# The end of the attention passes as one explicit list of single steps, with expert 0's early products between them

## The chip, the cores and the metric

The kernel runs on one core of one Trainium2 chip. The metric is the device time of one execution in microseconds (us). The core has five engines that run beside each other, each strictly in the order of its own program: PE (TensorE, matrix products), DVE (VectorE), ACT (ScalarE), POOL (GpSimd, which also issues the indirect DMAs) and SP (SyncE, which issues the other DMAs).

## The reference

```python
def _attn_ref(q, k, v):                       # 8 batches, 8 heads, 576 tokens, 64 features
    ...
    q_d = q.reshape(B, H, Sd, factor, D).mean(axis=3)     # factor 4; k_d and v_d likewise
    out_d = sm_attn(q_d, k_d, v_d)
    out_up = np.repeat(out_d, factor, axis=2)
    mask = np.abs(pos[:, None] - pos[None, :]) < factor
    scores = np.where(mask, scale * np.matmul(q, k.transpose(0, 1, 3, 2)), -1000000000.0)
    ...
    return (out_up + np.matmul(attn, v)).astype(np.float32)

def _moe_ref(x, w_gate, w1, w2):              # x: 4608 tokens of 512 features
    logits = x @ w_gate
    expert_idx = np.argmax(logits, axis=1)    # one of 8 experts
    ...
    for e in range(E):
        h = np.maximum(x_sorted[lo:hi] @ w1[e], 0.0)      # 512 -> 1024
        y_sorted[lo:hi] = h @ w2[e]                       # 1024 -> 512
    return (gate_w[:, None] * y).astype(np.float32)
```

A token attends to its neighbours at a distance below 4 and, on a coarse grid of means over 4 tokens, to all tokens of its batch. The sum of both is the input of a mixture of 8 experts, of which each token takes the one with the highest logit.

## The kernel before

**Attention** takes 32 passes; pass i handles two heads of one batch, four passes make a batch. A pass is cut into steps (local scores `s_loc`, their row maximum `max_loc`, the exponent `exp_loc`, row sums `sums`, `norm`, transposes `t_loc` and `t_d`, their copies out of PSUM `e_loc` and `e_d`, the products with the values `pv_loc` and `pv_d`, `out_d`, and `add_up`, which writes the pass's output into `XT`). The steps of neighbouring passes are interleaved: the table `PASS` holds (step, lag) pairs, and `steps(i)` emits every step for pass i minus its lag. So attention needs three more calls, `steps(32)` to `steps(34)`, to drain, and `steps(35)` for what follows them.

**Routing** works on groups of tiles of 128 tokens; a pair of batches m has nine tiles, taken as the first four (FIRST4) and the last five (LAST5). It runs in three parts: `route_a` (gate logits on PE, `r_mm`, and their copy `r_lg`), `route_b` (turn, maximum, one-hot of the winner) and `route_c` (`r_place` ranks the tokens within their expert on PE, `r_rk`, `r_pos`, then `r_ix` on POOL makes row numbers). `x_rows` transposes a tile of `XT` into token rows and `scatter` sends these with an indirect DMA to the expert's place in `xs` in DRAM.

**Expert 0 starts early.** Its first 256 rows (`EARLY`) are there before the last tokens are routed. They are loaded (`x_load(0, 0)`, four DMAs, L586), transposed on DVE (L617), split into a high part on ACT (L621) and a low part on DVE (L622), and go through the first layer as eight products `s1(0, f, EARLY)`: each has 12 PE instructions (L674 to L676), a copy on ACT (L678) and one on DVE (L679). The second layer needs both halves of w2 (`split_w2`: ACT L663, DVE L664). `s2(0, 0)` and `s2(0, 1)` (L688 to L690) finish the early tokens. The other 256 columns of expert 0, and all that follows, need `x_load(0, 1)`, which reads `xs` after every scatter has landed. While rows are being read from `xs`, no scatter may write it: the scatter behind `x_load(0, 0)` waits for that load.

What sets the order is the order in which the code emits the steps: each engine runs its share of them in that order, and a step that waits holds back all that stands behind it on its engine. PSUM banks set waits too: `bank()` has three, and transposes, logits and ranks share them.

Before the change, `x_load(0, 0)` stands at the end of pass 31; then come `steps(32)`, half of a routing group, two `x_rows`, the split of the early rows, `steps(33)`, the first product, the remaining passes, and then routing, scatters, products and w2 splits in whole functions (the block at the end of the main loop).

Of the kernel before, what the change touches and what calls it, by code (L numbers as in the profile page):

```python
# [90 lines left out]
def attention_moe_kernel(ctx: ExitStack, tc: tile.TileContext, qk, vw, vd, wg, w1, w2, cst, csb, out):  # L91
# [316 lines left out]

    def r_lg(m, tiles):
        lg = RS[m, "lg"] = rp.tile([128, 384], F32, name="over", bufs=1)  # L410
        w = 256 if len(tiles) == 4 else 384
        nc.scalar.activation(lg[:, :w], RS[m, "p"][:, :w], AF.Copy)

    def r_turn(m, tiles):
        lg = RS[m, "lg"]
        p = RS[m, "p"] = bank()
        for u in range(2):
# [5 lines left out]
    def r_max(m, tiles):  # L423
        T = len(tiles)
        RS[m, "pl"] = RS[m, "p"][:, :T * 32].rearrange("p (t e) -> p t e", e=32)[:, :, :E]
        RS[m, "m"] = rp.tile([128, 5], F32, name="rm")
        nc.vector.tensor_reduce(RS[m, "m"][:, :T], RS[m, "pl"], axis=AX.X, op=OP.max)

    def r_sub(m, tiles):
        T = len(tiles)  # L430
        d = RS[m, "d"] = RS[m, "p"][:, 256:296].rearrange("p (t e) -> p t e", e=E)
        nc.vector.tensor_sub(d[:, :T], RS[m, "pl"], RS[m, "m"][:, :T, None].to_broadcast([128, T, E]))

    def r_exp(m, tiles):
        T = len(tiles)
        ex = RS[m, "ex"] = rp.tile([128, 5, E], F32, name="re")
        nc.scalar.activation(ex[:, :T], RS[m, "d"][:, :T], AF.Exp)

    def r_top(m, tiles):
        T = len(tiles)  # L440
        sc = RS[m, "sc"] = RS[m, "p"][:, 320:360].rearrange("p (t e) -> p t e", e=E)
        nc.vector.scalar_tensor_tensor(sc[:, :T], RS[m, "d"][:, :T], 0.0,
                                       cf[:, None, C_DESC:C_DESC + E].to_broadcast([128, T, E]),
                                       op0=OP.is_ge, op1=OP.mult)

    def r_first(m, tiles):
        T = len(tiles)
        nc.vector.tensor_reduce(RS[m, "m"][:, :T], RS[m, "sc"][:, :T], axis=AX.X, op=OP.max)

    def r_hot(m, tiles):  # L450
        T = len(tiles)
        oh = RS[m, "oh"] = rp.tile([128, 5, E], BF, name="oh")
        nc.vector.tensor_tensor(oh[:, :T], RS[m, "sc"][:, :T], RS[m, "m"][:, :T, None].to_broadcast([128, T, E]),
                                op=OP.is_equal)

    def r_gate(m, tiles):
        T = len(tiles)
        gt = RS[m, "gt"] = rp.tile([128, 5], F32, name="gt")
        nc.vector.tensor_reduce(gt[:, :T], RS[m, "ex"][:, :T], axis=AX.X, op=OP.add)

    def r_eps(m, tiles):
        T = len(tiles)
        gt = RS[m, "gt"]
        nc.scalar.activation(gt[:, :T], gt[:, :T], AF.Copy, bias=1e-9)

    def r_place(m, tiles):
        T = len(tiles)
        oh = RS[m, "oh"]
        p = RS[m, "p"] = bank()
        nc.tensor.matmul(p[:, :T * E], trib, oh[:, :T], start=True, stop=False, skip_group_check=True)  # L470
# [6 lines left out]
    def r_cs(m, tiles):  # L477
        cs = RS[m, "cs"] = rp.tile([128, E], F32, name="cs")
        nc.vector.tensor_reduce(cs, RS[m, "oh"][:, :len(tiles)].rearrange("p t e -> p e t"), axis=AX.X, op=OP.add)

    def r_run(m, tiles):
        nc.gpsimd.tensor_add(crun, crun, RS[m, "cs"])

    def r_rk(m, tiles):
        T = len(tiles)
        rk = RS[m, "rk"] = rp.tile([128, 5, E], F32, name="rk", bufs=1)
        nc.vector.tensor_mul(rk[:, :T], RS[m, "p"][:, :T * E].rearrange("p (t e) -> p t e", e=E), RS[m, "oh"][:, :T])

    def r_pos(m, tiles):
        T = len(tiles)  # L490
        pos = RS[m, "pos"] = rp.tile([128, 5], F32, name="pos")
        nc.vector.tensor_reduce(pos[:, :T], RS[m, "rk"][:, :T], axis=AX.X, op=OP.add)

    def r_ix(m, tiles):
        T = len(tiles)
        ix = rp.tile([128, 5], I32, name="ix")
        nc.gpsimd.tensor_copy(ix[:, :T], RS[m, "pos"][:, :T])
        for j, t in enumerate(tiles):
            IDX[m, t] = ix[:, j:j + 1]

    def r_last(m, tiles):
# [3 lines left out]
        nc.scalar.copy(xrs[:, sl, DM + 1], cf[:, C_TOK + t0:C_TOK + t0 + T])  # L505
        nc.vector.reciprocal(xrs[:, sl, DM], RS[m, "gt"][:, :T])

# [11 lines left out]

    def x_rows(m, t):  # L520
        p = bank()
        for k in range(4):
            nc.tensor.transpose(p[:, k * 128:(k + 1) * 128], XT[m][:, k, t * 128:(t + 1) * 128], ident)
        xr = xrs[:, x_slot(m, t)]
        nc.scalar.activation(xr[:, :DM].rearrange("p (b k d) -> p k b d", k=4, d=32),  # L525
                             p.rearrange("p (k b d) -> p k b d", k=4, d=32), AF.Copy)

    prev_sc = []
# [151 lines left out]

# [232 lines left out]
    def steps(i):  # L913
        for f, lag in PASS:
            if 0 <= i - lag < NP:
                f(i - lag)

    load_vd(0)
    steps(-1)
    for i in range(NP):  # L920
        steps(i)
# [40 lines left out]
    x_rows(m, 4)  # L962
    split_w2(0, 0)
    s1(0, 3, EARLY)
    x_rows(m, 5)
    for f in (4, 5, 6, 7):
        s1(0, f, EARLY)
        if f == 4:
            for t in rest:
                scatter(m, t)  # L970
        for j in (2 * f - 7, 2 * f - 6):
            if j < 6:
                split_w2(0, j)
    totals()
    close_pv.close()
# [98 lines left out]
```

## Time and profile before

| | us |
|---|---|
| median of 3 runs | 649.36 |
| lowest and highest | 646.58, 651.08 |
| the profiled execution | 644.67 |
| its span, first to last instruction | 642.9 |
| PE busy, share of the span | 617.6, 96% |

The profile is one execution. Engine rows give start, duration, engine, line and operation. "x8" says that eight instructions in a row are merged. A row of the chain of waits is a piece of the work that ended last, each released by the one above it.

### The profile page before, as it was taken

The page shows a single profiled execution, that of the slowest core. Times are in us where ns is not written, and L with a number is a line of the kernel's source. Part 1 is how long each engine was busy: PE and PEld are TensorE (multiplying, and loading weights), DVE is VectorE, ACT ScalarE, POOL GpSimd, SP SyncE. Part 2 cuts the span into 40 slices and gives each one's busy share as a digit, 9 for nine tenths or more (in the row PEclk, how much of TensorE's full clock was granted, in tenths as well). Part 3 has the DMA queues.
Part 4 walks back from the last instruction along what each step waited for, and adds up shares of the span by engine and source line. Part 5 has one row for each costly group of instructions (what it writes and reads, how often), then busy time and mean ns, then how long its engine had stood idle before and what let it go on. Part 6 is the DMA issues. An engine that isn't in the chain of part 4 may idle for free.

```text
span 642.9 us, 15721 instructions
## 1 busy us (share of the span) xinstructions
PE 617.6 (96%) x6123; PEld 507.9 (79%) x6123; DVE 352.3 (55%) x691; ACT 343.3 (53%) x941; POOL 226.6 (35%) x348
## 2 busy tenths in 40 slices
PE   7899999999979899999999999999999999999994
PEld 4678887787768798888888888888888888888873
DVE  5999988888854573751571174175038166115020
ACT  4899999999964353543452263264235154223120
POOL 7877899999924311111111101101011111110111
PEclk9999999999989999999999999999999999999997
DMA  8998999999862794383274276258137537010001
GB/s 286 286 269 285 292 302 286 292 280 290 239 195 84 187 304 136 122 224 90 84 191 138 66 187 192 68 155 213 56 109 183 181 112 197 35 47 1 34 18 43
DMA packets 68612, 108.65 MB, mean 169 GB/s; under 512 B 15724, under 2 KB 39804, under 8 KB 68496
## 3 DMA queue, kind: packets, MB, share of 16 engines
q1 hardware_dynamic: 62080, 87.78, 49.0%
q0 software_dynamic: 5984, 19.01, 7.9%
q8 instruction: 66, 1.08, 0.8%
q14 instruction: 50, 0.41, 0.2%
q10 hardware_dynamic: 432, 0.37, 0.2%
HBM read 87.09 MB, written 23.67 MB: 172 GB/s over the span
## 4 chain that ended last, share of the span: by engine, by line
PE 68%; issue 10%; POOL 7%; DMA 5%; DVE 5%; ACT 2%; SPq 1%; POOLq 0%; another core or an unknown queue 0%; DVEq 0%; ACTq 0%
PE p L675 8%; PE p L674 8%; PE p L676 8%; PE p L690 7%; PE p L688 7%; PE p L689 7%; POOL xs L550 2%; DMA vd<-in_vd_dram 2%; PE pD L305 2%; POOL vdt L230 2%; PE pX L770 2%; PE pX L789 2%; PE pX L342 1%; PE pS L251 1%; PE pX L329 1%
## 5 line engine op out<-in xcount | busy, mean ns | idle before, releaser
L695 POOL DMA_INDIRECT out_dram<-y,tix x39 | 37.9, 971 | 213.3 <-ACT y L707 201.9
L674 PE MATMUL p<-xh,w1h 128*128 128x512 f32 (+1 forms) x288 | 106.4, 370 | 0.8 <-ACT xh L621 0.7
L675 PE MATMUL p<-xl,w1h 128*128 128x512 f32 (+1 forms) x288 | 105.7, 367 | 0.8 <-DVE xl L622 0.8
L676 PE MATMUL p<-xh,w1l 128*128 128x512 f32 (+1 forms) x288 | 105.5, 366 | 0.0
L688 PE MATMUL p<-w2h,hh 128*128 128x512 f32 x256 | 101.1, 395 | 0.0
L689 PE MATMUL p<-w2l,hh 128*128 128x512 f32 x256 | 99.8, 390 | 0.5 <-DVE w2l L664 0.5
L690 PE MATMUL p<-w2h,hl 128*128 128x512 f32 x256 | 99.9, 390 | 0.0
L679 DVE SCALAR_TENSOR_TENSOR hl<-p,hh 128x512 fp32r<-128x512 f32 (+1 forms) x72 | 45.5, 632 | 94.3 <-ACT hh L678 93.6
L678 ACT ACTIVATE hh<-p 128x512 fp32r<-128x512 f32 (+1 forms) x72 | 39.6, 551 | 78.1 <-PE p L676 75.6
L707 ACT ACTIVATE y<-p,gi 128x512 f32<-128x512 f32 x32 | 22.0, 689 | 91.2 <-PE p L690 86.8
L674 PEld LDWEIGHTS p<-xh,w1h 128*128 128x128 f32 x288 | 54.7, 190 | 10.7 <-ACT xh L621 1.1
L675 PEld LDWEIGHTS p<-xl,w1h 128*128 128x128 f32 x288 | 54.7, 190 | 9.6 <-DVE xl L622 0.9
L676 PEld LDWEIGHTS p<-xh,w1l 128*128 128x128 f32 x288 | 54.6, 190 | 8.7
L689 PEld LDWEIGHTS p<-w2l,hh 128*128 128x128 f32 x256 | 48.1, 188 | 10.6 <-DVE w2l L664 0.9
L690 PEld LDWEIGHTS p<-w2h,hl 128*128 128x128 f32 x256 | 48.1, 188 | 10.2
L688 PEld LDWEIGHTS p<-w2h,hh 128*128 128x128 f32 x256 | 48.1, 188 | 9.5
L664 DVE TENSOR_TENSOR w2l<-raw,w2h 128x512 fp32r<-128x512 f32 x64 | 43.3, 681 | 2.1 <-DMA xs<-xr,ix 1.5
L622 DVE TENSOR_TENSOR xl<-pX,xh 128x512 fp32r<-128x512 f32 x38 | 24.7, 684 | 35.2 <-ACT xh L621 34.2
L194 ACT ACTIVATE w1h<-raw 128x512 fp32r<-128x512 f32 (+1 forms) x72 | 42.1, 584 | 0.0
L550 POOL DMA_INDIRECT xs<-xr,ix x36 | 36.4, 1012 | 15.6 <-ACT xr L525 6.9
L663 ACT ACTIVATE w2h<-raw 128x512 fp32r<-128x512 f32 x64 | 39.8, 626 | 2.8 <-DMA xs<-xr,ix 2.8
L230 POOL TENSOR_TENSOR vdt<-vd 72x512 f32<-72x512 f32 x32 | 40.9, 1279 | 0.3
(152 smaller groups left out, 1240.1 us busy)
## 6 DMA issues: line engine op xcount, KB each, us to landing
raw<-in_w_dram SPq DMA_DIRECT2D x59, 512.0 KB
qk<-in_qk_dram SPq DMA_DIRECT2D x32, 583.0 KB
vw<-in_vw_dram SPq DMA_DIRECT2D x32, 320.0 KB
vd<-in_vd_dram SPq DMA_DIRECT2D x32, 288.0 KB
xrow<-xs SPq DMA_DIRECT2D x32, 192.0 KB
xrow<-xs SPq DMA_DIRECT2D x32, 128.0 KB
xs<-zs SPq DMA_DIRECT2D x6, 512.0 KB
raw<-in_w_dram SPq DMA_DIRECT2D x20, 128.0 KB
```

Source lines behind the costliest of these rows:

```text
L194: nc.scalar.activation(hi[:, s], src[:, s], AF.Copy)
L230: nc.gpsimd.tensor_add(t2, v[:, 0:2], v[:, 2:4])
L550: ins = nc.gpsimd.indirect_dma_start(out=xs, out_offset=bass.IndirectOffsetOnAxis(ap=IDX[m, t], axis=0), in_=xr, in_offset=None)
L663: nc.scalar.activation(hi, src, AF.Copy)
L664: nc.vector.tensor_sub(lo, src, hi)
L674: nc.tensor.matmul(p, wh[:, fs], xh[:, k, r], start=(k == 0), stop=False)
L675: nc.tensor.matmul(p, wh[:, fs], xl[:, k, r], start=False, stop=False)
L676: nc.tensor.matmul(p, wl[:, fs], xh[:, k, r], start=False, stop=(k == 3))
L679: nc.vector.scalar_tensor_tensor(hl[:, f, r], p, 0.0, hh[:, f, r], op0=OP.max, op1=OP.subtract)
L688: nc.tensor.matmul(p, hh, wh, start=(f == 0), stop=False)
L689: nc.tensor.matmul(p, hh, wl, start=False, stop=False)
L690: nc.tensor.matmul(p, hl, wh, start=False, stop=(f == 7))
```

## The change

1. `vw`, the values of a pass, gets three buffers instead of two.
2. `early_count`, which checks that expert 0 already has its 256 early rows, stands behind pass 28 instead of pass 29.
3. The main loop ends after pass 30. All that followed, from pass 31 to `totals`, becomes the table `TAIL` of 195 single steps in one written order. For that, functions that did several engines' work are cut into one step per engine: `x_rows` into `x_tr` (PE) and `x_ev` (ACT), `s1` into `s1_mm` (PE), `s1_hi` (ACT) and `s1_lo` (DVE), `split_w2` into `w2_hi` (ACT) and `w2_lo` (DVE), the split of the early rows into `x_up` (DVE), `x_hi` (ACT) and `x_lo` (DVE). The operations and their sizes stay.
4. The routing's scratch table is keyed by group as well, so that two groups can be under way.

```diff
-        VW[i] = p2.tile([128, NC, 2, D], F32, name="vw", bufs=2)
+        VW[i] = p2.tile([128, NC, 2, D], F32, name="vw", bufs=3)
...
-        p = RS[m, "p"] = bank()
+        p = RS[m, tiles[0], "p"] = bank()
...
-    def x_rows(m, t):
-        p = bank()
+    def x_tr(m, t):
+        p = BX["x", m, t] = bank()
...
+    def s1_mm(f):
+        s1_part(0, f, EARLY, 0)
+
+    def s1_hi(f):
+        s1_part(0, f, EARLY, 1)
+
+    def s1_lo(f):
+        s1_part(0, f, EARLY, 2)
...
+    TAIL = (
+        (max_d, 30), (x_tr, 2, 8), (exp_loc, 30), (eps, 29), (e_d1, 28), (x_tr, 3, 2), (s_loc, 31), (inv, 29),
...
-    for i in range(NP):
+    for i in range(NP - 1):
         steps(i)
...
         if i == 28:
             nc.sync.dma_start(cf[:, C_LIM:], cst[:, C_LIM:])
-        if i == 29:
             early_count()
-        if i == NP - 1:
-            close_p1.close()
-            close_s.close()
-            _, mp[0] = pool(name="m1", bufs=1)
-            _, mp["p1"] = pool(name="psM1", bufs=2, space=PSUM)
-            x_load(0, 0)
-            gi_load(0, 0, 2)
-            raw_ahead(8)
-    m = B // 2 - 1
-    first, rest = list(range(4)), list(range(4, 9))
-
-    steps(NP)
-    route_b(m, first)
-    x_rows(m, 2)
-    x_rows(m, 3)
-    prep(0, 0, 1, get=h_bank)
-    steps(NP + 1)
-    s1(0, 0, EARLY)
-    gi_make(0, 0, 2)
-    steps(NP + 2)
-    steps(NP + 3)
-    route_a(m, rest)
-    route_c(m, first)
-    for t in (2, 3, 0, 1):
-        scatter(m, t)
-    route_b(m, rest)
-    x_rows(m, 6)
-    x_rows(m, 7)
-    s1(0, 1, EARLY)
-    route_c(m, rest)
-    x_rows(m, 8)
-    s1(0, 2, EARLY)
-    x_rows(m, 4)
-    split_w2(0, 0)
-    s1(0, 3, EARLY)
-    x_rows(m, 5)
-    for f in (4, 5, 6, 7):
-        s1(0, f, EARLY)
-        if f == 4:
-            for t in rest:
-                scatter(m, t)
...
-    totals()
+    for f, *a in TAIL:
+        f(*a)
```

Three places show how instructions move. The first is PE, from the values' products of the last pass (L357 and L370) to the logits of LAST5 (L401 and L406) and what stands ahead of its ranks (L470). Before:

```order
L357 MATMUL pPV<-AT,vw 64x58 x20
L370 MATMUL pPV<-ADT,vds 64x144 x4
L401 MATMUL pX<-XT,wgt 32x256 x8
L406 MATMUL pX<-XT,wgt 32x128 x4
L470 LDWEIGHTS cb
L470 MATMUL pX<-oh,cb 128x32
```

Of the change (L697 is the last line of an early product, L676 before):

```order
L697 MATMUL p_4612<-xh_4316,w1l_3643 128x256
L401 MATMUL pX<-XT,wgt 32x256 x8
L406 MATMUL pX<-XT,wgt 32x128 x4
L523 MATMUL pX<-cf,XT 128x128 x4
L418 MATMUL pX<-cf,over 128x64 x2
L421 MATMUL pX<-cf,over 128x32
L523 MATMUL pX<-cf,XT 128x128 x4
```

A whole product stands ahead of the logits now, the ranks of FIRST4 (L470, 128x32) are gone from behind them, and the rows' transposes (L523) stand around the turn (L418).

The second is DVE around the row numbers of LAST5 (L492 before `r_ix`). Before:

```order
L459 TENSOR_REDUCE gt<-re 128x5
L679 SCALAR_TENSOR_TENSOR hl<-p_4629,hh 128x256
L479 TENSOR_REDUCE cs<-oh 128x8
L487 TENSOR_TENSOR rk<-pX,oh 128x40
L492 TENSOR_REDUCE pos<-rk 128x5
L506 RECIPROCAL xr<-gt 128x5
L679 SCALAR_TENSOR_TENSOR hl<-p_4668,hh 128x256
L664 TENSOR_TENSOR w2l_4696<-raw,w2h_4695 128x512
```

Of the change (L701 is L679 before, L677 is L664):

```order
L459 TENSOR_REDUCE gt<-re 128x5
L701 SCALAR_TENSOR_TENSOR hl<-p_4612,hh 128x256
L479 TENSOR_REDUCE cs<-oh 128x8
L487 TENSOR_TENSOR rk<-pX,oh 128x40
L492 TENSOR_REDUCE pos<-rk 128x5
L506 RECIPROCAL xr<-gt 128x5
L701 SCALAR_TENSOR_TENSOR hl<-p_4675,hh 128x256
L677 TENSOR_TENSOR w2l_4699<-raw,w2h_4698 128x512
```

The low part ahead of the ranks belongs to an earlier product now (p_4612 is the product ahead of the logits above), and two low halves of w2 follow instead of six.

The third is POOL between the two groups' row numbers (L497). Before:

```order
L605 CAST tix<-gi 128x2
L497 CAST ix<-pos 128x4
L482 TENSOR_TENSOR crun<-crun,cs 128x8
L549 MEMSET spacer 1x1
L550 DMA xs<-xr,ix 42112x514
```

Of the change (L556 and L557 are the same spacer and scatter):

```order
L612 CAST tix<-gi 128x2
L661 MEMSET tgi 128x2
L661 MEMSET ttix 128x1
L661 MEMSET gap 128x16
L497 CAST ix<-pos 128x4
L482 TENSOR_TENSOR crun<-crun,cs 128x8
L556 MEMSET spacer 1x1
L557 DMA xs<-xr,ix 42112x514
```

Before, two scatters of batch pair 2 stand ahead of L605 and four scatters follow L482; of the change, one stands ahead of L612 and five follow.

## Rows read from the trace of the kernel before

**Rows 1.** The chain of waits in 16 to 50 us: start, duration, what.
```profile
25.37 0.74 DVE mx L264
...
30.11 0.75 DVE mx L264
...
35.03 1.18 ACT AD L319 x6
```

**Rows 2.** Waits in 16 to 50 us: total, times, longest.
```profile
POOL qkt L219 <- DMA qk<-in_qk_dram: 6.5, 5, 1.8
```

**Rows 3.** SP's waits in 16 to 50 us.
```profile
SPq L211 <- PE pPV L357: 13.1, 5, 3.0
```

**Rows 4.** Busy time by stretch: PE, PEld, DVE, ACT, POOL, granted clock, DMA share, GB/s.
```profile
182.00:184.00 2.00, 0.82 (x8) 0.62 (x8) 1.09 (x7) 0.38 (x3) 0.00 (x0) 1.00 1.07 138
...
188.00:190.00 2.00, 1.90 (x11) 1.90 (x12) 0.83 (x2) 1.40 (x5) 0.00 (x0) 0.62 1.04 399
190.00:192.00 2.00, 2.00 (x12) 2.00 (x11) 0.00 (x0) 0.53 (x1) 0.00 (x0) 0.53 0.30 116
...
200.40:223.50 23.10, 22.41 (x143) 19.37 (x141) 11.40 (x30) 10.40 (x24) 10.27 (x22) 1.00 0.61 160
```

**Rows 5.** The chain of waits in 165 to 226 us.
```profile
167.52 0.60 PE pPV L357 x39
168.12 0.65 PE pPV L370 x8
168.77 0.69 PE pX L329 x5
169.47 0.44 PE pX L523 x4
...
195.05 0.84 DVE XT L385 x2
...
206.02 1.36 POOL xs L550
...
212.00 3.29 DMA xs<-xr,ix
...
217.03 4.92 DMA xrow<-xs
```

**Rows 6.** PE in order of time, pieces of 189 to 226 us.
```profile
190.13 0.56 PE L674 MATMUL p<-xh,w1h 128*128 128x256 f32 x1
...
192.43 0.45 PE L342 MATMUL pX<-cf,AD 112*72 112x112 f32 x3
...
196.39 0.39 PE L406 MATMUL pX<-XT,wgt 128*32 128x128 f32 x4
...
198.91 0.36 PE L674 MATMUL p<-xh,w1h 128*128 128x256 f32 x1
...
200.42 0.19 PE L470 MATMUL pX<-oh,cb 128*128 128x40 bf16 x1
...
223.04 0.39 PE L690 MATMUL p<-w2h,hl 128*128 128x512 f32 x1
...
225.22 0.38 PE L675 MATMUL p<-xl,w1h 128*128 128x256 f32 x1 [0.75 <-DVE xl L622]
```

**Rows 7.** DVE in order of time: the early rows' transposes.
```profile
183.97 1.32 DVE L617 STREAM_TRANSPOSE p<-xrow 128x512 f32<-128x512 f32 x2 [0.19 <-DMA xrow<-xs]
```

**Rows 8.** ACT in order of time, pieces of 179 to 197 us.
```profile
185.00 1.08 ACT L621 ACTIVATE xh<-p 128x512 fp32r<-128x512 f32 x2
...
194.61 0.41 ACT L374 ACTIVATE outd<-pPV 128x288 f32<-128x288 f32 x1 [0.96 <-PE pPV L370]
```

**Rows 9.** POOL in order of time, pieces of 201 to 204 us.
```profile
201.20 0.97 POOL L550 DMA_INDIRECT xs<-xr,ix  x1 [0.22 <-issue]
202.48 0.97 POOL L550 DMA_INDIRECT xs<-xr,ix  x1 [0.22 <-DVE xr L506]
203.46 0.20 POOL L497 CAST ix<-pos 128x5 int32<-128x5 f32 x1
```

More of the change, by code (lines that the diff above doesn't have):

```diff
@@ L467, in r_place @@
         T = len(tiles)
-        oh = RS[m, "oh"]
-        p = RS[m, "p"] = bank()
+        oh = RS[m, tiles[0], "oh"]
+        p = RS[m, tiles[0], "p"] = bank()
         nc.tensor.matmul(p[:, :T * E], trib, oh[:, :T], start=True, stop=False, skip_group_check=True)
@@ L526, in x_rows @@
                              p.rearrange("p (k b d) -> p k b d", k=4, d=32), AF.Copy)
+    def x_rows(m, t):
+        x_tr(m, t)
+        x_ev(m, t)
     prev_sc = []
@@ L916, in steps, with shut, x_in, gi_in @@
                 f(i - lag)
+    XP = {}
+    def shut():
+        close_p1.close()
+        close_s.close()
+        _, mp[0] = pool(name="m1", bufs=1)
+        _, mp["p1"] = pool(name="psM1", bufs=2, space=PSUM)
+    def x_in():
+        x_load(0, 0)
+        XH[0, 0] = tuple(mp[0].tile([128, 4, FIRST], F32R, name=f"x{w}0") for w in "hl")
+        HT[0] = tuple(mp[0].tile([128, 8, FIRST], F32R, name=f"h{w}") for w in "hl")
+    def gi_in():
+        gi_load(0, 0, 2)
+    def w2_in():
+        raw_ahead(8)
@@ new lines, in s1_lo, with w2_hi, w2_lo @@
+    def s1_lo(f):
+        s1_part(0, f, EARLY, 2)
+    def w2_hi(f):
+        w2_open(0, f)
+        w2_part(0, f, 0)
+    def w2_lo(f):
+        w2_part(0, f, 1)
+    TAIL = (
+        (max_d, 30), (x_tr, 2, 8), (exp_loc, 30), (eps, 29), (e_d1, 28), (x_tr, 3, 2), (s_loc, 31), (inv, 29),
+        (r_mm, 3, FIRST4), (x_ev, 2, 8), (t_d0, 28), (max_scale, 30), (x_ev, 3, 2), (norm, 29), (inv_d, 29),
+        (x_tr, 2, 7), (exp_d, 30), (max_loc, 31), (s_d, 31), (sub_loc, 31), (norm_d, 29), (r_lg, 3, FIRST4),
+        (r_turn, 3, FIRST4), (x_ev, 2, 7), (sums, 30), (exp_loc, 31), (x_tr, 3, 3), (pv_loc, 28), (r_max, 3, FIRST4),
+        (pool_v2, 30), (scatter, 2, 6), (e_d0, 28), (max_d, 31), (pool_v, 31), (pool_v2, 31), (shut,), (x_in,),
+        (r_sub, 3, FIRST4), (pv_d, 28), (r_top, 3, FIRST4), (eps, 30), (inv_d, 30), (x_ev, 3, 3), (inv, 30),
+        (norm_d, 30), (r_first, 3, FIRST4), (r_hot, 3, FIRST4), (t_loc1, 29), (e_loc1, 29), (norm, 30), (gi_in,),
+        (r_place, 3, FIRST4), (r_rk, 3, FIRST4), (t_d1, 29), (out_d, 28), (t_d0, 29), (x_up, 1), (add_up, 28),
+        (e_d1, 29), (e_d0, 29), (t_d1, 30), (e_d1, 30), (x_up, 0), (x_hi, 1), (x_lo, 1), (scatter, 2, 8), (ld_vw, 30),
+        (t_loc0, 29), (t_d0, 30), (r_pos, 3, FIRST4), (max_scale, 31), (e_loc0, 29), (e_d0, 30), (x_hi, 0), (x_lo, 0),
+        (t_loc1, 30), (exp_d, 31), (pv_d, 29), (pv_loc, 29), (t_loc0, 30), (out_d, 29), (w2_in,), (r_exp, 3, FIRST4),
+        (sums, 31), (gi_out,), (e_loc0, 30), (x_tr, 3, 1), (eps, 31), (e_loc1, 30), (inv, 31), (inv_d, 31),
+        (x_ev, 3, 1), (r_ix, 3, FIRST4), (norm_d, 31), (s1_mm, 2), (w2_hi, 0), (norm, 31), (s1_hi, 2), (s1_mm, 3),
+        (add_up, 29), (t_loc1, 31), (e_loc1, 31), (t_loc0, 31), (r_cs, 3, FIRST4), (r_gate, 3, FIRST4), (pv_d, 30),
+        (r_eps, 3, FIRST4), (out_d, 30), (s1_lo, 2), (e_loc0, 31), (s1_hi, 3), (pv_loc, 30), (x_tr, 3, 0), (t_d0, 31),
+        (r_run, 3, FIRST4), (t_d1, 31), (e_d0, 31), (scatter, 2, 7), (r_last, 3, FIRST4), (e_d1, 31), (ld_vw, 31),
+        (add_up, 30), (pv_loc, 31), (x_ev, 3, 0), (w2_lo, 0), (pv_d, 31), (out_d, 31), (scatter, 3, 0), (add_up, 31),
+        (w2_hi, 2), (w2_lo, 2), (w2_hi, 5), (s1_lo, 3), (s1_mm, 6), (w2_hi, 1), (scatter, 3, 3), (r_mm, 3, LAST5),
+        (w2_lo, 1), (w2_hi, 4), (r_lg, 3, LAST5), (x_tr, 3, 5), (x_ev, 3, 5), (w2_lo, 5), (r_turn, 3, LAST5),
+        (r_max, 3, LAST5), (r_sub, 3, LAST5), (scatter, 3, 2), (s1_hi, 6), (r_top, 3, LAST5), (r_first, 3, LAST5),
+        (r_hot, 3, LAST5), (x_tr, 3, 8), (s1_mm, 0), (r_exp, 3, LAST5), (r_gate, 3, LAST5), (x_ev, 3, 8), (s1_lo, 6),
+        (scatter, 3, 1), (r_cs, 3, LAST5), (w2_hi, 3), (r_place, 3, LAST5), (r_eps, 3, LAST5), (r_rk, 3, LAST5),
+        (r_run, 3, LAST5), (r_pos, 3, LAST5), (r_ix, 3, LAST5), (s1_hi, 0), (r_last, 3, LAST5), (s1_lo, 0),
+        (w2_lo, 3), (w2_lo, 4), (x_tr, 3, 4), (x_ev, 3, 4), (s1_mm, 5), (s1_hi, 5), (s1_mm, 1), (s1_lo, 5),
+        (scatter, 3, 5), (x_tr, 3, 7), (s1_hi, 1), (x_ev, 3, 7), (s1_lo, 1), (x_tr, 3, 6), (s1_mm, 4),
+        (scatter, 3, 4), (x_ev, 3, 6), (s1_mm, 7), (scatter, 3, 8), (scatter, 3, 7), (s1_hi, 4), (totals,),
+        (s1_lo, 4), (s1_hi, 7), (s1_lo, 7), (scatter, 3, 6),
+    )
```

118 lines of the change are left out of this document (70 added, 48 removed).

## The prediction

> **What bounds the kernel now.** I read the views in this order: the chain of waits, for which stretches can be shortened at all; the waits of SP and POOL, for what the third `vw` buffer could free; then the chain again around the end of attention, with each engine's rows in order of time.
>
> The whole span is 96% PE. What is left sits in two places. In passes 4 to 9 the chain repeats every 4.74 us on a DVE instruction, 25.37 and 30.11 [rows 1]: DVE sets the pace there. The second place is the end of attention. The chain [rows 5] runs through the last passes' products to `add_up(31)` (195.05 + .84 = 195.89), through routing to the last five scatters (the first starts at 206.02, the last is over at 212.97), through the last scatter's landing (212.00 + 3.29 = 215.29; the load behind it has left before 217.03), and through the load of the second half of expert 0's rows (217.03 + 4.92 = 221.95). DVE transposes these rows, and PE takes them up at 225.22 [rows 6]. From then on the program is the same instructions in the same order, so whatever time the start of the second half gains or loses, the end gains or loses.
>
> Beside that chain PE has other work: the early products, then the early second layer, which ends at 223.04 + .39 = 223.43 [rows 6]. So PE is idle for only 1.8 us before the second half, and the filler is a second limit that sits close behind the first.
>
> **The third vw buffer.** SP's wait for the values' buffer, 13.1 us in 16 to 50 us [rows 3], goes. It delays loads queued behind it, and the only consumer late for a load there is POOL, 6.5 us in five waits for qk [rows 2]. But the chain in that stretch is DVE's [rows 1], fed by PE and ACT, and no row of POOL stands on it. I take 0. Bounds: 0, and as much as a quarter of POOL's waits, −1.5, if one or two of the five reach DVE.
>
> **early_count one pass earlier.** The same few instructions, moved across one pass that PE fills. 0.
>
> **The tail, up to add_up(31).** The rows of the early tokens arrive at 183.97 [rows 7]; what stands before that on POOL (`pool_v2`, `scatter(2, 6)`) and on SP keeps its order, so they arrive then again. Before, the passes' steps did not stand behind them. Now they do: `x_up` heads DVE's queue with `add_up(28)`, `sums(31)` and `norm(31)` behind it, `x_hi` heads ACT's with `exp_d(31)` behind it, and through these PE waits too. From the rows: two transposes of .66 [rows 7] with an `add_up` of .84 [rows 5] between them end at 186.1; `x_hi` .54 [rows 8], `exp_d(31)` 1.18 [rows 1], `out_d(29)` .41 [rows 8] and the small `r_exp`, whose bank the next transpose takes (.2, as the copy of five columns took) [rows 9], end at 188.4. PE then has `x_tr` .44 [rows 5], two early products of 1.51 (198.91 to 200.42) [rows 6], `t_loc(31)` .69, `pv_d(30)` .65, then `out_d(30)` .41, for whose reading `pv_loc(30)` waits, .60, transposes of about 1.15 (one `x_tr` and `t_d`), `pv_loc(31)` and `pv_d(31)` 1.25, `out_d(31)` .41 and `add_up(31)` .84 [rows 5, 8]. 188.4 + .44 + 3.02 + .69 + .65 + .41 + .60 + 1.15 + 1.25 + .41 + .84 = 197.86, against 195.89: **+1.95**. Before, only one product stood ahead of these steps, and it took 190.13 to 192.43 [rows 6], 2.30 for the same instructions.
>
> **From there to the first scatter.** The logits stood .9 behind `add_up(31)` (end 196.78). Now the product `s1_mm(6)` is ahead of them and ends behind `add_up(31)`; I take 1.4: **+.5**. Logits to ranks took 3.64 (196.78 to 200.42) with a product between [rows 6]; a product stands there still, and the ranks of FIRST4 are gone from DVE and PE: 3.2, **−.4**. Ranks to row numbers took 3.0, as POOL sent four scatters of 1.28 each first, the last two from 201.20 and 202.48, so `r_ix` came at 203.46 [rows 9]. Now those four stand further ahead; the copy, two DVE steps and `r_ix` come to 1.1: **−1.9**. From there to the first scatter took 2.56 (206.02 − 203.46), as its rows were transposed late; in the new order `x_ev` of tile 5 is long done, and spacer and descriptor issue leave .7: **−1.8**.
>
> **The five scatters** took 206.02 to 212.97, 6.95. Two on [rows 9] start 1.28 apart and take .97; the first of the five took 1.36 [rows 5], with a low half of w2 (L664, two inputs from SBUF) on DVE beside it. Six such halves stood near the five; now two stand behind `s1_lo(0)`. Bounds: 4 × 1.28 + .97 = 6.09 and 6.95; I take 6.5, **−.45**. The Trainium skill, SBUF — State Buffer, section Who interferes with whom, says that a DVE instruction with two SBUF inputs contends with a GpSimd instruction that reads SBUF; the 1.36 against .97 agrees, and by it alone the term would lie at the lower bound, about −.85.
>
> **The clock.** PE's granted clock was 1.00 at 182 to 184 us, where PE was busy .82 of 2 us, and .62 and .53 at 188 to 192 [rows 4], in part the level of 1.2 GHz, although PE was nearly full there. That is the 2.30 instead of 1.51. The new order leaves PE with nothing at all between its last step ahead of the rows and about 186, when DVE has turned them, before it starts two products, so a low stretch comes again, and now other steps stand in it. Bounds: 0, and 1.6, two products at .79 each. I take **+.3**, as `pv_d(29)`, `pv_loc(29)` and transposes of some 2 us run before the products and take most of the low stretch, beside waits for ACT and DVE.
>
> **Loads and queues.** `ld_vw(30)` and `ld_vw(31)` stand behind `x_in` and `gi_in` in SP's queue now; their consumers `pv_loc(30)` and `pv_loc(31)` run 8 us and more behind, longer than the 4.92 that the row load took [rows 5]. Hidden; without that cover, up to 2 us. Scatter `(2, 8)` waits for `x_in`'s reading, as its neighbours did; POOL is then idle enough.
>
> **Sum.** 1.95 + .5 − .4 − 1.9 − 1.8 − .45 + .3 = **−1.8**. Landing, load and transposes follow unchanged. The filler must allow it: the ranks come at 202.5 by the sum (197.86 + 1.4 + 3.2), and behind them stands what took 200.42 to 223.43 before, less two products that now run ahead: 23.0 − 3.0 = 20.0, so it ends at 222.5, or at 221.8 without the .7 in which PE was idle there (22.41 busy of 23.10) [rows 4]. That permits a start 2.7 to 3.4 earlier. The profiled execution of 644.67 becomes 642.9. The median of the runs shown, 649.36, lies 4.7 higher, and the same change makes it **647.5**.
>
> **Rivals.**
>
> *PE becomes the limit* (.2). If scatters run at their lower bound, the first starts at once and no low clock meets the chain, the chain offers up to 4 us, and the start of the second half is set by the filler: −3.4, 646.0. The filler itself can end earlier if the steps ahead of the ranks close up; those hold about 1.4 of waits for ACT and DVE (two `out_d` of .41, half a microsecond at the splits), which makes −4.8: 644.6. For it: the spacing of 1.28 on [rows 9]. Against it: ranks to scatter pass through five small steps on three engines, each of which can wait behind a longer one.
>
> *No net gain* (.17). What the routing saves, the chain to `add_up(31)` loses, since three early products now stand ahead of the logits where one stood. If `s1_lo` and the w2 halves on DVE, or their high halves on ACT, hold back two or three small steps of .4 to .8, the sum is within 1 of zero: 649.4. This is also the case in which the change does what it says and POOL still comes late. For it: ACT and DVE hold .5 to 1.3 us pieces in that stretch [rows 7, 8].
>
> *A longer low clock* (.13), the case on the slower side. Place: PE from 186 to 199. Before, PE did odd work while it waited for the rows [rows 4]; now it does none. If the 1.2 GHz level then holds through the three products ahead of the logits and the last passes' products, it costs 3 × .79 = 2.4 for the products and, at the same ratio 2.30/1.51, about 2.4 for 4.7 us of other PE steps on the chain. With the .3 in the sum replaced: −2.1 + 4.8 = +2.7, 652.1. It decides once the low level covers work of more than 2.1/.52 = 4.0 us at full clock. For it: [rows 4] show the low level behind a stretch in which PE was even in part busy. Against: there it lasted about 4 us, two stretches. The Trainium skill, TensorE: Matmul & The Clock Gate, section Why this matters for your kernels, advises against idle gaps between bursts of products because the clock falls back to half; that speaks against this change, and [rows 4] agree that a fall comes, if not for how long.
>
> **How the numbers follow.** Forecast .5 (−3 to −1: 646.4 to 648.4), PE the limit .2, no net gain .17, low clock .13. About 1%, 6.5 us, is what a measurement here can tell from no change, and the runs before spread over 646.6 to 651.1 themselves, so a median moves by a microsecond or two on its own. The range: low 643.5, the filler's −4.8 with the buffer's part bound of −1; high 651.4, which takes in no gain with the spread and most of the low clock's case. Faster by over 1% (below 642.9) would need −4.8, the buffer's −1.5 and a lucky median: .09. Slower by over 1% (above 655.8) needs the low clock and a late load: .05. Within: .86.
>
> **What would show it.** Right: rows at about 184; `add_up(31)` over at about 197.9; `r_ix` of LAST5 at about 203.6 with POOL waiting for it rather than sending; the first scatter within 1 of it; the last over at about 210.9; the second half of the rows on DVE at about 220, PE's first use of them at about 223.2; the period 4.74 unchanged in passes 4 to 9 with SP's wait gone. Wrong: early products of 2.3 instead of 1.5 up to 199 (low clock), PE going from the early second layer into the second half without a wait (PE the limit), or `r_ix` behind a DVE step of w2 (no net gain). A pass period below 4.7 would make the buffer's term wrong.

## The result and the profile after

The change made the kernel slower. Over 19 runs each, the median is 651.02 us (647.61 to 656.38) against 646.58 (643.56 to 651.11; the 649.36 given ahead was of three of these runs), a ratio of 1.0068 with a 95% interval of 1.0041 to 1.0096: some 4.4 us. The forecast was 1.8 us faster. The profiled execution of the changed kernel took 654.68 us with a span of 652.9, so it is one of the slower ones; its stretches are read for where time goes, the size of the loss is taken from the runs.

Measured at the marks of the prediction, in that profile: the early rows are on DVE at 193.30 instead of 183.97 [rows 7], 9.3 late; PE multiplies the low part of the second half from 234.92 instead of 225.22 [rows 6], 9.7 late; from there to the end both need 418 us (417.7 before). So nearly all of this profile's loss lies *ahead* of the tail, in passes where the change only added a buffer, and the tail gave nothing.

**The passes.** The chain of waits of the changed kernel in 30 to 42 us (start, duration, what) shows the largest piece:

```profile
34.21 0.56 PE pS L251 x40
34.77 0.11 PE pPV L357 x6
34.88 3.13 issue
38.01 1.22 PE pPV L357 x24
39.23 1.16 PE pPV L370 x8
40.40 1.26 PE pX L329 x5
```

PE stops in the middle of `pv_loc`, after 6 of 40 instructions, for 3.13 us, and no row releases it ("issue"). Behind the stop the same steps take 1.16 and 1.26 instead of .65 and .69 [rows 5]: the clock has fallen too (granted .50 in 38 to 42 us). The same DVE step (L264) of this pass and the next starts 9.91 us apart instead of 4.75, so this stop costs about 5 us. The DMA trace of 35 to 37 us (queue, packets, MB, share) has beside it

```profile
q8 instruction: 1, 0.02, 3.7%
```

which is one 16 KB load of instructions, 35.2 to 36.4; the page counts 66 of them in the whole span, in the passes one for every 250 or so of PE's instructions (weight loads counted). The one before began at 27.4, 357 instructions earlier, where neighbours lie about 250 apart.

The waits in 20 to 165 us (total, times, longest), with two lines that answer to [rows 2]:

```profile
POOL qkt L219 <- DMA qk<-in_qk_dram: 7.2, 6, 2.5
PE pPV L357 <- issue: 7.1, 4, 3.1
```

In the kernel before, the second of these is `0.6, 2, 0.4`, the first 6.5. And SP's waits in 16 to 50 us, for [rows 3]:

```profile
SPq L207 <- POOL vdt L230: 7.9, 5, 2.4
SPq L119 <- PE pS L251: 4.6, 2, 4.3
```

The wait of 13.1 us for the vw buffer is gone, as forecast, but SP's waiting is not: it stands at qk's and vd's loads now, with one more vw load already under way.

**The tail.** Stretches of the changed kernel (PE, PEld, DVE, ACT, POOL, granted clock, DMA share, GB/s), for [rows 4]:

```profile
192.00:194.00 2.00, 0.00 (x0) 0.00 (x0) 0.70 (x2) 0.00 (x0) 0.00 (x0) 0.99 1.02 273
194.00:196.00 2.00, 0.80 (x4) 0.47 (x6) 2.00 (x6) 1.89 (x6) 1.29 (x5) 0.50 1.00 370
196.00:198.00 2.00, 2.00 (x46) 1.62 (x47) 1.43 (x3) 1.07 (x6) 0.19 (x1) 0.50 0.98 291
198.00:200.00 2.00, 2.00 (x21) 1.70 (x17) 0.21 (x2) 1.31 (x5) 0.00 (x0) 0.50 0.83 325
200.00:202.00 2.00, 2.00 (x16) 2.00 (x15) 1.81 (x7) 1.91 (x6) 0.13 (x1) 0.80 0.01 2
```

PE was idle 191.53 to 195.20, and then worked at the 1.2 GHz level until about 201. Its chain (for [rows 5]) in that stretch and to the scatters:

```profile
193.30 0.74 DVE p L624
...
194.11 0.60 ACT xh L969
...
194.80 0.36 ACT AT L336
...
195.20 0.69 PE pX L329 x2
195.89 1.17 PE pPV L370 x8
197.05 1.27 PE pPV L357 x40
198.32 0.83 PE pX L329 x3
199.16 0.90 PE pX L523 x4
...
203.29 0.55 PE pX L329 x5
203.84 0.68 PE pPV L370 x8
...
204.54 0.42 ACT outd L374
...
205.00 0.81 PE pPV L357 x40
...
216.48 1.00 POOL xs L557
...
221.61 3.33 DMA xs<-xr,ix
```

DVE and POOL in order of time give the two marks between, the end of `add_up(31)` and `r_ix` of LAST5 (for [rows 9]):

```profile
208.92 0.83 DVE L385 TENSOR_TENSOR XT<-pPV,outd 128x290 f32<-128x290 f32 x2 [1.54 <-ACT outd L374]
```

```profile
215.47 0.19 POOL L497 CAST ix<-pos 128x5 int32<-128x5 f32 x1 [0.27 <-DVE pos L492]
```

Counted from the rows' arrival, `add_up(31)` ends 16.4 behind it (11.9 before), `r_ix` comes 5.7 behind that (7.6 before), the last scatter is over 7.1 behind `r_ix` (9.5 before), and the second half follows in 12.3 (12.3). +4.5 − 1.9 − 2.4 = +.2, and +.4 with the .1 of the last step and the rounding: in this profile the tail is where it was.

### The profile page after: what moved, and what is told of

It reads as the page before. It is cut to its first block, busy times and chain, and to the rows that moved or that the text cites. A ratio compares the mean times of both kernels' runs of the same rounds, so it can differ in the third digit from the quotient of the medians.

```text
span 652.9 us, 15739 instructions
## 1 busy us (share of the span) xinstructions
PE 621.7 (95%) x6120; PEld 510.6 (78%) x6123; DVE 350.1 (54%) x691; ACT 343.7 (53%) x941; POOL 226.0 (35%) x348
## 4 chain that ended last, share of the span: by engine, by line
PE 76%; issue 9%; DMA 5%; ACT 3%; POOL 2%; DVE 2%; SPq 1%; POOLq 0%; another core or an unknown queue 0%; DVEq 0%; ACTq 0%
PE p L695 8%; PE p L696 8%; PE p L697 8%; PE p L710 7%; PE p L712 7%; PE p L711 7%; PE pD L305 4%; PE pX L329 3%; PE pX L342 3%; PE pPV L357 2%; PE pPV L370 2%; PE pS L251 2%; PE pX L523 2%; DMA xs<-xr,ix 2%; PE pX L792 2%
## 5 line engine op out<-in xcount | busy, mean ns | idle before, releaser
L697 PE MATMUL p<-xh,w1l 128*128 128x512 f32 (+1 forms) x288 | 105.5, 366 | 0.0
L701 DVE SCALAR_TENSOR_TENSOR hl<-p,hh 128x512 fp32r<-128x512 f32 (+1 forms) x72 | 45.4, 631 | 87.6 <-ACT hh L699 87.3
L697 PEld LDWEIGHTS p<-xh,w1l 128*128 128x128 f32 x288 | 54.5, 189 | 9.0 <-issue 0.2
L712 PEld LDWEIGHTS p<-w2h,hl 128*128 128x128 f32 x256 | 48.0, 188 | 10.2
L677 DVE TENSOR_TENSOR w2l<-raw,w2h 128x512 fp32r<-128x512 f32 x64 | 43.3, 680 | 0.9 <-DMA xs<-xr,ix 0.9
L629 DVE TENSOR_TENSOR xl<-pX,xh 128x512 fp32r<-128x512 f32 x38 | 24.6, 683 | 35.2 <-ACT xh L628 34.2
L557 POOL DMA_INDIRECT xs<-xr,ix x36 | 35.9, 997 | 18.0 <-DMA gi<-xs 5.8
```

Of the source, the lines that this page charges most:

```text
L701: nc.vector.scalar_tensor_tensor(hl[:, f, r], HP.pop((e, f)), 0.0, hh[:, f, r], op0=OP.max, op1=OP.subtract)
L712: nc.tensor.matmul(p, hl, wh, start=False, stop=(f == 7))
```

## Experiments

Ratios are against the kernel before on the same chip, with 95% intervals. Each run's profile is one execution. Two theories stood against each other. Theory 1: the third vw buffer lets SP send loads earlier, PE's own instruction loads come late behind them, and PE stops; the tail's gain went into the low clock. Theory 2: the buffer is harmless, and the tail alone is slower.

**One part alone, and the whole without it.** `b_vw3` is the kernel before with

```diff
-        VW[i] = p2.tile([128, NC, 2, D], F32, name="vw", bufs=2)
+        VW[i] = p2.tile([128, NC, 2, D], F32, name="vw", bufs=3)
```

> The kernel before with the third vw buffer alone. Theory 1 (the buffer lets SP send loads earlier, PE's own instruction loads get late behind them, and PE stalls in the middle of pv_loc with nothing to wait for): most of the 4.4 us that the change lost come with it, +3 to +6 us against the kernel before, with PE stalls of 1 us and more inside L357 or L251 in the passes. Theory 2 (the buffer is harmless, 0 as forecast; the loss is the low clock in the tail, and the passes of the one profile were an accident): within 1 us of the kernel before.

Measured: 1.0063 (1.0030 to 1.0095), some 4 us, as theory 1 had it, with stops of 1.38 (L251), 1.12 and .81 (L357) in its profile. `a_vw2` is the changed kernel with the opposite edit.

> The whole change without the third vw buffer. Theory 1: the passes are as before, the tail gives +0.4 us by the profile (9.7 us late at the second half, 9.3 of them there when the early rows arrive), so 0 to +1 us against the kernel before, and no PE stall over 1.2 us ahead of 165 us. Theory 2: +3 to +5 us, as with the buffer.

Measured: 1.0037 (1.0012 to 1.0063), 2.4 us: more than theory 1 allowed, less than theory 2 asked for. Its profile has no stop of .8 us in 20 to 165 us, but one pass of 8.9 us in which PE came through `pv_loc` in small pieces. Both were slower than the kernel before, and together they are more than the whole change: with about .3% of uncertainty each, that needed the four kernels on one chip:

> The kernel before again, fourth corner, which tells how far the same program lies from itself: within 0.15% of the kernel before. A third profile of it: s_d(31) between 176 and 181 us, s_d(28) to the second half 60.4 us, and PE stalls of .8 us and more ahead of s_d(31) of 1 to 3 us in all.

> The kernel before with three vw buffers again, third corner. Theory 1: +2 to +5 us against the kernel before, by stalls ahead of s_d(31), and the stretch from s_d(28) to the second half as before (60.4 to 60.8 us). If the buffer is harmless: within 1 us of the kernel before.

> The changed kernel with two vw buffers again, second corner. Theory 1: 2 to 4 us less than the corner with three buffers. If the buffer is harmless and the stalls come and go with the build and the run: within 1 us of that corner.

> The changed kernel again, as one corner of a square of four kernels on one chip: tail before or after, two or three vw buffers. Theory 1 (third buffer: late instruction loads; tail: a low clock that eats its gain): tail and buffer each add, +3 to +6 us against the kernel before, PE stalls that nothing releases of 3 us and more in all ahead of s_d(31).

(The 60.4 us in two of these are counted from s_d(29); from s_d(28) it is 66.)

| | two buffers | three buffers |
|---|---|---|
| order of before | 0.9994 (0.9968 to 1.0020), 651.57 us | 1.0043 (1.0010 to 1.0076), 654.78 us |
| order of the change | 1.0012 (0.9980 to 1.0044), 652.17 us | 1.0064 (1.0034 to 1.0093), 654.99 us |

The third buffer costs 3 us in either row, the new order about 1 us, which cannot be told from none here (`a_vw2` above was clear of none). In `f_before_vw3` the stretch from s_d(28) to the second half is 66.3 us, against 66.1, 66.0 and 68.9 in three profiles of the kernel before: its loss lies in the passes. In the waits of 20 to 165 us, PE's unreleased stops in L357 and L251 sum to 5.2, 9.7, 8.9 and 5.7 us in the four profiles with three buffers, and to 1.1 to 8.0, mean 4.0, in ten with two; in an eleventh, `f_after_vw2`, whose profiled run of 657.62 was the longest of its twelve, they sum to 8.2. POOL's wait for qk does not grow (6.9 to 10.2 against 6.5 to 11.9).

From the start of s_d(2) to that of s_d(28), passes that are the same program but for the buffer, the four profiles with three buffers took 147.5 to 155.9 us, mean 151.5, the eleven with two 142.0 to 153.6, mean 147.3. Of the 4.3 us between the means, PE's stops that nothing releases make 3.3 (7.4 against 4.1), and the low clock behind them some .4. So the buffer is not harmless, and theory 2 falls; a small loss by the new order, beside the buffer's, is not excluded.

A second profile of the kernel before, to see how far single profiles scatter:

> The kernel before once more, for a second profile of it. Theory 1 (PE's instruction loads get late behind SP's loads, more often with the third vw buffer): it has such stalls too, but fewer, so pass 31's s_d starts within 4 us of 176.4, and the sum of PE stalls of .8 us and more that nothing releases lies under 3.5 us ahead of 165 us (1.0 in the first profile, 7.1 in the changed kernel's). If single profiles scatter as widely as the two kernels differ, s_d of pass 31 comes at 180 or later.

Its s_d(31) starts at 179.0 (before: 176.4; `f_before`: 181.5, just outside the 176 to 181 expected), with two stops of together 2.2 us and one of .79. The kernel before has such stops as well, and its three profiles are longer in the order of their sums (2.2, 4.0 and 4.5 us; spans of 642.9, 645.0 and 649.7).

**Are the stops instruction loads?** `a_shift` puts 60 small products into the warm-up of the changed kernel:

```diff
     warm(WARM[0])
+    for _ in range(60):
+        nc.tensor.matmul(wp[:, :64], wsrc[:, :128], wsrc[:, :64], start=True, stop=True)
```

> The changed kernel with 60 small products (120 PE instructions with their weight loads) put in the warm-up ahead of all passes. Theory 1: PE stalls where its loaded instructions end, which is a place in its program counted from the start, so the stalls of the early passes move some 120 instructions ahead in the pass, off L357 (pv_loc) to L329, L305 or L342 or the end of L251; a 16 KB instruction load starts within 1.5 us of each. Theory 2 (they come from data that pv_loc or its neighbours wait for): they stay in L357.

PE in order of time, with the idle time ahead in brackets (L307 is `s_d`, L344 is `t_d`):

```profile
34.90 0.74 PE L307 MATMUL pD<-qkd 64*64 64x144 f32 x3 [1.96 <-issue]
81.09 0.67 PE L344 MATMUL pX<-cf,AD 112*72 112x112 f32 x5 [1.17 <-issue]
121.13 0.70 PE L307 MATMUL pD<-qkd 64*64 64x144 f32 x7 [1.24 <-issue]
139.67 0.58 PE L307 MATMUL pD<-qkd 64*64 64x144 f32 x6 [1.98 <-issue]
```

Not one long stop is left in `pv_loc` or `s_loc`; they moved to steps that read other data, and sit inside groups again. A wait for data would have stayed. It is a place in PE's program, counted from its start.

The DMA traces say the same. In all twenty profiles together, 44 of PE's stops in 20 to 165 us last .8 us or more and have no releaser. Each of them ends 1.29 to 1.74 us after one of q8's 16 KB loads is over, though these loads come about 5 us apart. In the changed kernel the load is over at 36.35 and PE goes on at 38.01, 1.66 later. In `a_shift` the loads began .6 to 1.6 us ahead of its four stops, nearly as expected. So q8's loads are taken for PE's instructions here, and the stops for the wait for them.

**Is it traffic?** `b_thin_vd` and `b_thin_vd3` load half of vd:

```diff
-        nc.sync.dma_start(VD[i].rearrange("p r c h d -> p (r c h d)"), vd[i])
+        nc.sync.dma_start(VD[i].rearrange("p r c h d -> p (r c h d)")[:, :512], vd[i][:, :512])
...
-        nc.gpsimd.tensor_add(t2, v[:, 0:2], v[:, 2:4])
+        nc.gpsimd.tensor_add(t2, v[:, 0:2], v[:, 0:2])
```

> The kernel before with half of vd's load left out (144 of 288 KB per pass; the means of v take the first two rows of each four twice, so the result differs). If PE's instruction loads are late because of the loads' traffic: fewer stalls, s_d(31) at 172 to 176 us, 1 to 4 us faster than before. If traffic is not the cause: no change.

> The same with three vw buffers. If the third buffer costs through traffic that stands ahead of the instruction loads: it costs less than 1.5 us now against the thin kernel with two buffers. If it costs by something else, it still costs 3 us.

`b_fat` adds a load that nobody reads:

```diff
+        if 3 <= i < 31:
+            junk = p1.tile([128, 256], F32, name="junk", bufs=2)
+            nc.sync.dma_start(junk, w2[7, (i % 4) * 128:(i % 4) * 128 + 128, :256])
```

> The kernel before with one more load of 128 KB in each of passes 3 to 30, into a tile that nobody reads. If the traffic of loads makes PE's instruction loads late: +3 to +8 us, with more and longer stalls inside L357 and L251 although nothing waits for this load. If only the bytes on the way to a consumer count: within 1 us in passes 11 to 31 and at most +2 us in all, from the loads behind it in SP's queue.

Measured: `b_thin_vd` 0.9880 (0.9839 to 0.9920), 640.77 us; `b_thin_vd3` 0.9927 (0.9899 to 0.9954), 642.78 us; `b_fat` 1.0100 (1.0065 to 1.0135), 654.08 us against 646.99. The waits in 20 to 165 us, of `b_thin_vd`

```profile
POOL qkt L219 <- DMA qk<-in_qk_dram: 7.2, 5, 1.9
PE pPV L357 <- issue: 0.7, 1, 0.7
```

and of `b_fat`:

```profile
POOL qkt L219 <- DMA qk<-in_qk_dram: 14.7, 11, 2.8
PE pPV L357 <- issue: 4.8, 5, 1.6
PE pS L251 <- issue: 2.9, 4, 1.1
```

144 KB less per pass is worth 6 us, more than the 1 to 4 expected, and nearly clears the stops; the kernel before has 2.2, 4.0 and 4.5 us of them in three profiles, so they are not all of the 6. 128 KB more costs 7, with 7.7 us of stops. qk comes late for POOL more often too, but PE's products show no wait for POOL there. (`b_fill` below, with the passes of before, has 8.0 us of stops in its one profile, so 7.7 alone would not show it.) On the thin kernel the third buffer costs 2.0 us (642.78 − 640.77); with intervals of .3 to .4% either way this is told neither from the 3 us elsewhere nor from the 1.5 of the expectation. So traffic costs time, and with less of it the stops nearly go; that it is their only cause is not shown.

`b_qk2` takes a buffer away elsewhere (`name="qk", bufs=3` to `bufs=2`).

> The kernel before with two qk buffers instead of three, so that SP sends qk's load a pass later. If the depth of what SP has sent ahead makes the instruction loads late: fewer stalls than the kernel before; but qk may then come late for POOL and PE, which wait for it: between -2 us (depth alone) and +8 us (qk late by some .3 us in each pass).

Measured: 1.0094 (1.0068 to 1.0119), 653.49 us, with 16.0 us of POOL's waits for qk and stops of 1.05, 1.29 and 1.86 in L357. Sending less far ahead did not clear the stops and made qk late. A plain "the deeper the queue, the later the instructions" is not borne out.

**The low clock.** `a_vw2_fill` and `a_fill2` put products without use where PE waits for the early rows:

```diff
+    def fill(n):
+        for _ in range(n):
+            nc.tensor.matmul(PD[31][:, 448:512], onesf, cf[:, :64], start=True, stop=True, skip_group_check=True)
...
-        (t_loc0, 29), (t_d0, 30), (r_pos
+        (t_loc0, 29), (t_d0, 30), (fill, 32), (r_pos
```

> The change with two vw buffers, and 11 products without use (fp32, 192 columns, some 3.5 us) on PE behind t_d0(30), where PE waits for the early rows. If the low clock behind that wait is what the tail's gain went into, the granted clock stays at 1.00 from 182 to 196 us and the kernel is 2 to 3 us faster than the change with two buffers. If the clock is not what costs there, within 0.5 us of it, or slower by what the products take longer than the wait.

This one wrote into the bank that `add_up(28)` reads, so the products waited for the rows themselves: 1.0111 (1.0061 to 1.0162), it tells nothing on the clock. The second:

> The change with two vw buffers, and 32 products without use (fp32, 64 columns, some .11 us each, 3.4 us) behind t_d0(30) that nothing on another engine holds up, so that PE is busy until the early rows are split. If the low clock in the steps behind that wait is the tail's loss: the granted clock stays at 1.00 there, add_up(31) ends 2 to 3 us earlier measured from the rows' arrival (13.5 to 14.5 instead of 16.4), and the kernel is 2 to 3 us faster than the change with two buffers was, -0.1% to 0.1% against the kernel before. If the clock is not the cause, no change to the change with two buffers, +0.2% to +0.6%.

Measured: 1.0048 (1.0024 to 1.0073). Stretches and chain of `a_fill2`:

```profile
186.00:188.00 2.00, 2.00 (x21) 2.00 (x19) 1.63 (x4) 0.19 (x1) 1.35 (x6) 1.00 1.04 395
188.00:190.00 2.00, 2.00 (x56) 1.63 (x55) 0.00 (x0) 1.20 (x6) 0.00 (x0) 1.00 0.37 145
190.00:192.00 2.00, 1.86 (x29) 1.56 (x19) 0.69 (x3) 1.74 (x6) 0.00 (x0) 1.00 0.34 83
```

```profile
181.48 7.11 PE pD L993 x64
188.59 0.22 PE pX L329 x2
188.81 0.65 PE pPV L370 x8
189.46 0.78 PE pPV L357 x40
```

The clock stayed at 1.00, and from `t_loc1(30)` to the end of `add_up(31)` PE's chain took 12.4 us (188.42 to 200.80) where the changed kernel took 14.5 (195.20 to 209.74). All of the difference lies ahead of the next L329 (5.77 against 7.93 us), where PE never waits in either; behind it both take 6.6. So the clock is worth 2.2 us there. But the filling took .22 us a product instead of .11 and ended 7.11 us later, some 3.0 us behind the time the rows could be used (183.50, and 1.9 for the split as in the changed kernel, is 185.4; PE came at 188.4 with the transposes). So `add_up(31)` ended 17.3 behind the rows, not the 13.5 to 14.5 expected: what the clock gave back, the filling took. So the clock's price is shown, a gain from keeping it up is not.

`b_fill` does the same in two waits of the kernel before (9 products of 64 columns behind the first `x_rows`, 3 of 192 between `pv_loc(30)` and `pv_d(30)`):

> The kernel before with such products in two of its waits, 9 of 64 columns behind the first x_rows of the end and 3 of 192 columns (.32 us each) between pv_loc(30) and pv_d(30). If the clock falls because PE waits there, and it costs the stretch behind it: the granted clock stays at 1.00 in 188 to 192 us instead of .62 and .53, the first early product takes 1.5 instead of 2.3, and the kernel is 1 to 2 us faster than before. If not, no change.

Measured: 1.0038 (1.0012 to 1.0063). The granted clock was 1.00 from 180 to 220 us, `add_up(31)` ended 10.8 instead of 11.9 behind the rows, and from s_d(28) to the second half it took 66.1 us, as in two of the three profiles of before: the scatters and loads behind set that end. Its profile has stops of 1.12, 2.83, 1.60 and 1.83 us in passes that are the same program as before. Timed runs have no trace, so why they are slower too is open.

**Another order.** In `a_vw2_last` the steps on the early rows and the products 2 and 3 stand behind the passes' steps that don't need them:

```diff
-        (t_d1, 29), (out_d, 28), (t_d0, 29), (x_up, 1), (add_up, 28),
+        (t_d1, 29), (out_d, 28), (t_d0, 29), (add_up, 28),
...
+        (x_ev, 3, 1), (r_ix, 3, FIRST4), (norm_d, 31), (norm, 31), (x_up, 1), (add_up, 29), (x_up, 0),
+        (x_hi, 1), (x_lo, 1), (x_hi, 0), (x_lo, 0), (t_loc1, 31), (e_loc1, 31), (t_loc0, 31), (e_loc0, 31),
+        (pv_d, 30), (out_d, 30), (r_cs, 3, FIRST4), (r_gate, 3, FIRST4), (s1_mm, 2), (r_eps, 3, FIRST4), (w2_hi, 0),
```

> The change with two vw buffers, and the steps that need the early rows (x_up, x_hi, x_lo, the products 2 and 3) moved behind the steps of passes 29 to 31 that don't. If the wait of about 3.7 us at the head of the queues, with the low clock behind it, is the tail's loss, then PE has passes' work while the rows come, add_up(31) ends 3 to 5 us earlier, and the kernel is 2 to 4 us faster than the change with two buffers; the filler work may then be the limit. If the chain through DVE and ACT between passes 29 and 31 is the limit, within 1 us of it.

Measured: 1.0016 (0.9981 to 1.0051), .2% less than `a_vw2`, not told from it. PE's one long wait became four of .33 to 1.06 us, which DVE and ACT released, and the clock fell behind these (.55 and .60 in 196 to 200 us). This is the expectation's second case, the chain through DVE and ACT as the limit.

`h` keeps the order of before up to `add_up(31)` and takes only what gained behind it:

```diff
     x_rows(m, 3)
+    route_c(m, first)
     prep(0, 0, 1, get=h_bank)
...
     gi_make(0, 0, 2)
+    for t in (2, 3, 0, 1):
+        scatter(m, t)
...
     x_rows(m, 8)
+    x_rows(m, 4)
+    x_rows(m, 5)
     s1(0, 2, EARLY)
+    for t in (6, 7, 8, 4, 5):
+        scatter(m, t)
```

> The kernel before, with route_c(FIRST4) ahead of prep, its four scatters behind gi_make, and the rows of tiles 6, 7, 8, 4, 5 and their scatters ahead of the w2 splits. If the changed kernel's gain behind add_up(31) is real and its loss ahead of it comes from the steps that wait for the early rows: add_up(31) ends 12 us behind the rows' arrival as before, the second half's rows come 3 to 4 us earlier, PE's early second layer then ends after them, and the kernel is 1 to 2 us faster than before. If the gain behind add_up(31) needs the whole new order: no change.

> The same with products without use in two of PE's waits (4 of 64 columns, .22 us each as measured, behind the first x_rows; 2 of 192 columns between pv_loc(30) and pv_d(30)). If the low clock costs the filler 1.5 us there: granted clock 1.00 through 186 to 196 us, the early second layer ends 1 to 2 us earlier, 2 to 3.5 us faster than before. If not: as h.

Measured: `h` 0.9987 (0.9957 to 1.0017), 645.85 us against 646.84; `h_fill` 1.0002 (0.9975 to 1.0029). In `h` the second half's rows come 22.6 us behind `add_up(31)` instead of 26.2, as expected, and the early second layer now runs into the second half without a wait: PE has become the limit, and the gain ends there: the 1.0 us between the medians is not told from none. `h_fill` takes up the second half 64.5 us behind s_d(28) instead of 66.1, and its profile shows the next loss, a PE stop of 2.2 us at 412.8 (it ends 1.42 us after an instruction load). No version that loads all its data was measured faster than the kernel before.

## Why the prediction was wrong

**The third buffer, taken as 0, is the step that failed.** The bounds were 0 and −1.5; a loss was excluded because only POOL waited for loads, and POOL was not on the chain. The runs put +3 us in its place. Whom a load can delay was asked of the engines' data alone; PE's instruction loads, one line of the page's DMA part, are counted there on the same 16 DMA engines and were left out. The runs show that the stops sit where PE's program has got to and end with an instruction load, that they nearly go with less traffic, and that the buffer costs 3 us. That the buffer costs by these stops is likely (they make 3.3 of the 4.3 us by which the profiles differ on average), but the two ranges overlap. With the +.4 of the tail, 3.4 of the 4.4 us are accounted for.

**The clock, taken as +.3, measured 2.2.** The wait and the fall came as described; the choice near the lower bound failed. The idle time was 3.7 us, and the low level held for some 7 us, over all steps that followed and into the first product, where the prediction reckoned with the 4 us seen before and with other steps in most of it. The measured price lies above its bound of 1.6, since that counted the two products alone. This is the rival of the longer low clock in its place, at less than its full price of 4.8. The Trainium skill, TensorE: Matmul & The Clock Gate, section Why this matters for your kernels, had advised against such gaps; the stretch 192 to 200 us agrees.

**The chain to `add_up(31)`** without the clock was forecast at 13.9 us behind the rows; 1.9 + 12.4 = 14.3 is what the runs make of it. That it is right within .4 is in part luck: `x_tr` was to wait for ACT's `r_exp`, 4.4 behind the rows, but PE's own steps of passes 29 and 30 took until then, and in the profile after ACT waited 1.32 for PE.

**Routing and scatters were right in this profile.** Forecast −1.8 to `r_ix` (.5 − .4 − 1.9) and −2.25 from there to the last scatter's end; measured −1.9 and −2.4. The two w2 low halves on DVE (from 215.91) lay beside the first of the last five scatters alone, which took 1.00, the others .97; all started 1.3 us apart. A low half beside a scatter does not always lengthen it: before, the second of the five (207.69) took .97 although one ran on DVE from 207.93. Landing, load and transposes followed unchanged, and 417.4 to 420.6 us remained behind the start of the second half in every kernel.

**The passes' period:** with SP's wait gone, L264 started at 20.78, 25.54, 30.47 and 35.22, so 4.75 came back, as forecast, until the long stop. The spread of the first three runs, 4.5 us, had been noted, but not asked for its cause.

**Two readings to set right.** The three runs that the forecast of 647.5 was added to had a median 2.8 us above that of all nineteen; that 651.02 lies inside the range of 643.5 to 651.4 is owed to this. And PE does not take up the second half at 225.22, it goes on with it there; it began with the high part:

```profile
224.08 0.38 PE L674 MATMUL p<-xh,w1h 128*128 128x256 f32 x1 [0.66 <-ACT xh L621]
```

So PE was idle there for .66 + .75 = 1.4 us, not 1.8, and the filler stood that much closer.

Open is a wait of 2.3 us on ACT ahead of the logits' copy (L412), in four of the eight profiles with the new order, of kernels with two and with three buffers. In `f_after`, with what PE makes of it:

```profile
210.14 0.49 ACT L412 ACTIVATE over<-pX 128x384 f32<-128x384 f32 x1 [2.31 <-PE pX L523]
```

```profile
210.69 1.11 PE L418 MATMUL pX<-cf,over 128*128 128x64 f32 x4 [2.02 <-ACT over L412]
```

against .31 in the profile after; PE's last logit was out 2.1 us before the copy. Another low clock follows (.50 in 212 to 216 us). In these four `r_ix` comes 8.7 to 10.2 behind `add_up(31)`, later than the 7.6 of before, so the routing's gain is lost in them; in the other four it comes 5.7 to 6.5 behind. From s_d(28) to the second half they take 69.0 to 70.6 us, the profile after 66.6. This may be what the new order loses beside the buffer's 3 us; no run here explains the wait.

## What to carry to other kernels

Where a stretch keeps the DMA engines 90% busy (.92 to 1.00 in 40 to 160 us here), a buffer that only lets loads go earlier need not be free: ask what else uses these engines, instruction loads among it, and look for stops with no releaser inside a group of like instructions, then for an instruction load that is over just before each ends. Moving the program by a hundred instructions tells such a stop from a wait for data. A wait of PE that was taken together into one gap cost twice here, by its 3.7 us and by the 2.2 us of clock behind it. A gain that is laid against a second limit close behind, here PE's other work with 1.4 us to spare, ends at that limit.

## What was not expected of the hardware

PE's instructions came in 16 KB loads that took .9 to 1.6 us each in the changed kernel. When one came late PE stood for 1 to 3 us, and went on 1.3 to 1.7 us after the load was over. 128 KB per pass that nobody reads, a tenth of the traffic, cost 1.0% of the kernel's time, and 144 KB less gave 1.2%.
